# Seven block products for batch 1's second product, with other places for sums of w_out, for the scaling of second probabilities and for batch 3's softmax

## The chip, the cores and the metric

One NeuronCore of a Trainium2 chip runs the kernel. TensorE (PE) multiplies, VectorE (DVE), ScalarE (ACT) and GpSimd (POOL, Pool) work elementwise, SyncE (SP) issues most DMA transfers; each engine takes its own instructions in order. The metric is the device time of one execution in microseconds. Before the change the median of three runs was 206.49 us (206.39 to 206.8).

## The reference

x is (8, 8, 512, 64): batch, head, row, width; state is (8, 8, 32, 64). Two softmax attentions share their scores, and their results, stacked to 544 rows of 512 per batch, go through a two-layer product with a leaky ReLU.

```python
scale = 1.0 / np.sqrt(D)
scores = scale * np.matmul(x, state.transpose(0, 1, 3, 2))
scores = scores - scores.max(-1, keepdims=True)
a = np.exp(scores)
a /= a.sum(-1, keepdims=True) + 1e-09
xread = np.matmul(a, state)
scores2 = scale * np.matmul(state, x.transpose(0, 1, 3, 2))
scores2 = scores2 - scores2.max(-1, keepdims=True)
a2 = np.exp(scores2)
a2 /= a2.sum(-1, keepdims=True) + 1e-09
sread = np.matmul(a2, x)
attn = np.concatenate([xread, sread], axis=2)
x = attn.transpose(0, 2, 1, 3).reshape(B * S, H * D)   # S is 544 here
h = x @ w_in                                            # 512 x 2048
return np.maximum(0.01 * h, h) @ w_out                  # 2048 x 512
```

## The kernel before

Everything is in bf16 with sums in fp32. For a batch b the first product folds state and w_in together: M = state times w_in (`a_m`, four column groups of 512, numbered 0 to 3 here), so that the hidden layer is M applied to the first probabilities `aT`. M group c is computed into PSUM (tile `pm`) and copied to SBUF by `m_evict`.

The loop over s, 0 to 15, makes one 128-column block of the hidden layer per step: `ff1` runs two matmuls of 512 columns into a bank "ph" (two buffers, used in turn) and ScalarE's Prelu (L352) writes `hT[:, s]`. Each ff1 must wait until the Prelu two steps earlier, or whatever else used its bank, has emptied it.

Between the ff1 stand pieces of the second product, hT times w_out, of the batch before or of this batch. There are two ways of doing it:
- `piece(b, hT, i, jq)`: four matmuls of 512 columns for row block i and quarter jq of the depth, into a bank "py". 16 pieces make a batch; `y_store` copies a finished row block and sends it out. Batches 0 and 1 use this.
- `Batch` with `Fast`: the product is cut in 2 x 2 blocks, rows (256 + 256), depth (even and odd blocks of 128) and columns (256 + 256), and done with seven block products in place of eight. `Fast.sums` makes four sums of blocks of hT on VectorE (`su`, L511); `weights_sum` makes four sums of blocks of w_out (`tw`, L488, once for the kernel; sum 1 reads sum 2 and sum 3 reads sum 1). A unit (n, m) is two matmuls of 256 columns (L522), seven n times eight m for a batch. The products accumulate in two banks "py", in the order 1, 2, 6, 5, 7, 3, 4: 1, 6, 7 and 4 in the first, 2, 5, 3 in the second. Between them `save` copies a bank to SBUF on ScalarE (`sv`, L531) and `join` adds a bank to a saved block on VectorE (`yo`, L534). Batches 2 to 7 use this: 15 units of a batch run at the end of its own loop, 41 in the loop of the next, spread over the steps by `PACE`.

Other PSUM tags: "sc", one buffer of two banks, holds scores and sometimes a group of M; "big", one buffer of two banks, holds groups of M and the state reads (`psr`, L299).

Attention of the next batch is woven into the same loop: `a_scores` (TensorE), `a_shift` and `a_max2` (VectorE: transposed maximum L215, spread L223, subtraction L225, row maximum L265), `a_exp` and two `a_exp2` (ScalarE, L232 and L273), `a_probs` (VectorE, L237 to L247, writes `aT`), `a_probs2` (VectorE, L279 to L284: scales the second probabilities), `a_a2t` (a DMA transpose on SyncE's queue), `a_sread` (TensorE, then two ScalarE copies L306). `cast_x` makes bf16 of x on Pool (L105). a0, a1, a2 are the attention objects of batches 0 to 2.

The order of all instructions on each engine is the order in which the code issues them; semaphores follow from the tiles. So an instruction that waits holds all behind it on its engine.

Batch 1's loop is L858 to L885, the loops of batches 2 to 7 are L891 to L989. In batch 2's loop the ten remaining pieces of batch 1 are done at steps 0 to 9, groups 0, 1 and 2 of batch 3's M are computed after step 10, and group 2 is copied out of two "ph" banks by VectorE and ScalarE (L987):

```python
for g, copy in enumerate((VEC, SCA)):
    copy(nxt.M[:, g, 2 * DM:3 * DM], pm2[g][:])
```

Of the kernel before, what the change touches and what calls it, by code (L numbers as in the profile page):

```python
# [9 lines left out]
P = 128  # L10
# [17 lines left out]
def kernel(  # L28
# [248 lines left out]

    def a_probs2(a):
        nc.vector.tensor_scalar(out=a.r2[:], in0=a.r2[:], scalar1=1e-9, scalar2=None, op0=ALU.add)  # L279
        q2 = att.tile([P, 2], FP32, name="qc", tag="qc")  # L280
        nc.vector.reciprocal(q2[:], a.r2[:])
        a.a2 = att.tile([P, 2, S], BF16, name="a2", tag="a2")
        for g in range(2):
            nc.vector.tensor_scalar(  # L284
                out=a.a2[:, g, :], in0=a.e2[:, g, :],
                scalar1=q2[:, g:g + 1], scalar2=None, op0=ALU.mult,
            )

    def a_a2t(a):
# [54 lines left out]
    def ff1(a, hT, j):  # L344
        ph = psum.tile([P, S], FP32, name="ph", tag="ph")
        for g in range(2):
            nc.tensor.matmul(  # L347
                ph[:], lhsT=a.M[:, g, P * j:P * (j + 1)],
                rhs=a.aT[:, g, :],
                start=(g == 0), stop=(g == 1),  # L350
            )
        nc.scalar.activation(out=hT[:, j, :], in_=ph[:], func=AF.Prelu, alpha=0.01)  # L352


# [185 lines left out]
    class Batch:  # L540
        def __init__(self, b, hT):
            saved = {n: (spool, t, 1) for n, t in ((1, "sv1"), (6, "sv6"), (5, "sv1"), (7, "sv7"))}
            self.b, self.f = b, Fast(hT, 2 * P, [(spool, f"su{n}", 1) for n in range(4)], saved)
            self.units = [(n, m) for n in (1, 2, 6, 5, 7, 3, 4) for m in range(NM)]
            own = [(n, m) for n in (1, 2) for m in range(6)] + [(1, 6), (2, 6), (1, 7)]
            assert len(own) == OWN
            self.units = own + [u for u in self.units if u not in own]
            self.bank = {}
            self.yos = {}
# [22 lines left out]
        def run(self, count):  # L572
            f = self.f
            for _ in range(count):
                n, m = self.units.pop(0)
                if m == 0:
                    self.open(n)
                bank = self.bank[n]
                f.unit(bank, n, m, first=n in (1, 2, 5, 4))
                if m == NM - 1:  # L580
                    self.done(n, bank)

        def done(self, n, bank):
# [16 lines left out]
            elif n == 4:  # L600
                f.join(self.yo(1)[:, :, :HC], bank, 7)
                self.out(1)

    OWN = 15
    PACE = (1, 4, 4, 4, 3, 4, 4, 3, 4, 4, 4, 4, 3, 4, 3, 3)
    PACE2 = (0,) * 10 + (3, 3, 2, 2, 2, 3)

# [235 lines left out]
    open_xb(3)  # L843
    a_probs(a1)
    for i in range(NT):
        piece(0, h0, i, 2)
    for i in (2, 3):
        piece(0, h0, i, 3, copy=None)
    for i in (2, 3):
        y_store(0, i, VEC)  # L850
    for h in range(0, H, 2):
        cast_x(3, h, h + 2, POO)
# [5 lines left out]
    h1 = hpool.tile([P, 16, S], BF16, name="hT", tag="hT")  # L858
    fill = [(0, h0, 0, 3), (0, h0, 1, 3)] + [(1, h1, i, jq) for jq in range(3) for i in range(2)]
    for s in range(16):  # L860
        ff1(a1, h1, s)
        if s % 2:
            pb, hT, i, jq = fill[s // 2]
            piece(pb, hT, i, jq, copy=VEC if s == 3 else SCA)
        if s == 4:
            a_scores(a2)
            m_evict(a2, 0, a_m(a2, 0, "big"), SCA)
            a_shift(a2)
            a_max2(a2)
        elif s == 7:  # L870
            a_exp(a2)
            a_open(att_of[3], 3)
            a_xt_dma(att_of[3])
        elif s in (9, 11):
            a_exp2(a2, s // 2 - 4)
            if s == 9:
                a_probs(a2)
            else:
                a_probs2(a2)
        elif s == 13:  # L880
            a_probs2(a1)
            a_a2t(a1)
            pm = [a_m(a2, 1, "big"), a_m(a2, 2, "sc")]
            m_evict(a2, 1, pm[0], VEC)
            m_evict(a2, 2, pm[1], SCA)  # L885

    before = None
    weights_open()  # L890
    for b in range(2, B):  # L891
# [3 lines left out]
        now = Batch(b, hT)  # L895
        std = []
        if b == 2:
            std = [(i, 3) for i in range(2)] + [(i, jq) for i in range(2, NT) for jq in range(4)]

        def fill(s):  # L900
            n = (PACE2 if b == 2 else PACE)[s]
            left = min(n, len(before.units)) if before else 0
            if left:
# [4 lines left out]
        for s in range(16):  # L908
            if s == 11:
                fill(s)  # L910
            ff1(a, hT, s)
            if s == 0:
# [3 lines left out]
                a_a2t(a)  # L916
                if before:
                    for n in (0, 1):
                        before.f.sums(n, 4, 8)
            elif s == 1:  # L920
                if nxt is not None:
                    a_scores(nxt)
# [3 lines left out]
                if b + 2 < B:  # L926
                    for h in range(0, H, 2):
                        cast_x(b + 2, h, h + 2, POO)
                if before:
                    before.f.sums(2, 4, 8)  # L930
            elif s == 3:
                if before:
                    before.f.sums(3)
                if nxt is not None:
                    a_max2(nxt)
                if b == 2:
                    weights_sum(0)
                    weights_sum(2)
            elif s == 4:
                if b == 2:  # L940
                    load_state(1)
                    a_sread(a0)
            elif s == 6:
                if b == 2:
                    a_sread(a1)
            elif s == 8:
                a_sread(a)
                if b == 2:
                    state_t(1)
                    weights_sum(1)  # L950
                    weights_sum(3)
            elif s == 12:
                for n in range(3):
                    now.f.sums(n, 0, 4)
            if nxt is None:
                if s == 4:
# [3 lines left out]
                elif s == 10:  # L960
                    fi.w_sum(3)
                    fi.x_sums()
            if s == (11 if b == 2 else 7) and b + 2 < B:
                a_open(att_of[b + 2], b + 2)
                a_xt_dma(att_of[b + 2])
            if nxt is not None:
                if s == 5:
                    a_exp(nxt)
                elif s in (7, 8):
                    a_exp2(nxt, s - 7)  # L970
                    if s == 7:
                        a_probs(nxt)
                elif s == 11:
                    a_probs2(nxt)
                elif s in (12, 13):
                    SCA(nxt.M[:, s - 12, DM:2 * DM], pm1[:, s - 12, :])
            if std:
                i, jq = std.pop(0)
                piece(1, h1, i, jq)
            elif s != 11:  # L980
                fill(s)
            if s == 10 and nxt is not None:
                pm0 = a_m(nxt, 0, "big")
# [96 lines left out]
```

## Time and profile before

| what | value |
|---|---|
| median of three runs | 206.49 us |
| the profiled execution, its time | 206.1 us |
| its span, first to last instruction | 204.3 us |
| granted TensorE clock | 1.000 |
| ScalarE's Prelu of an ff1, L352, 112 | 603 ns each |
| ScalarE's exponential, L232, 128x1024, 7 | 1050 ns each |
| ScalarE's half exponentials, L273, 16 | 693 ns each |
| VectorE's half sums of hT, L511, 128x1024, 24 | 694 ns each |
| Pool's casts of x, L105, 128x512, 20 | 790 ns each |
| window 36.78 to 52.61 us (batch 1's loop): PE, DVE, ACT, POOL busy | 15.37, 13.83, 12.77, 2.30 us |
| window 52.61 to 74.61 us (batch 2's loop): PE, DVE, ACT, POOL busy | 22.00, 18.30, 18.14, 5.36 us |

A line of a timeline gives start, duration, engine, line and operation of the code, output and input by the program's names, sizes, and in brackets the idle time of that engine just before and what ended it. Matmuls overlap, so their rate is read from start to start; the ends of matmuls are modelled. Instructions in a row on one engine are merged with a count. The chain of waits follows the work that ended last back to its start.

### The profile page before, as it was taken

Reading aid. Unit: us, or ns where it says so; the run is one execution under the profiler, and the core shown is the slowest. Engines: PE = TensorE matmul, PEld = TensorE weight load, DVE = VectorE, ACT = ScalarE, POOL = GpSimd, SP = SyncE. Lnnn points to the kernel's source line nnn. Section 1 sums busy time; section 2 is a strip of 40 time slices with the busy share of each in tenths; the row PEclk is TensorE's granted clock in tenths of the full one; section 3 lists DMA queues with packets and bytes.
Section 4 is the critical chain, followed back from the end, with each engine's and each line's share of the span. In section 5 each row is a group of like instructions: output and inputs, shape, how many; then the busy total and the mean of one; then the engine's idle time right before and its main releaser. Section 6 shows DMA issues by size and latency. Waiting matters only on the chain.

```text
span 204.3 us, 4533 instructions
## 1 busy us (share of the span) xinstructions
PE 198.0 (97%) x1852; PEld 126.8 (62%) x1852; DVE 152.3 (75%) x231; ACT 145.2 (71%) x274; POOL 41.8 (20%) x66
## 2 busy tenths in 40 slices
PE   7899999999999999999999999999999999999992
PEld 2543534443445557766776767776767677799882
DVE  1677689599699969966996699679978763686622
ACT  3359848578959796978787878788778856467710
POOL 8921002021035103500402040200020002004250
PEclk9999999999999999999999999999999999999999
DMA  5999994799456498549452769250016000410035
GB/s 188 223 207 280 227 253 134 147 305 218 104 179 176 128 194 176 53 155 269 95 103 106 209 152 106 99 160 5 0 47 210 3 3 22 183 55 0 3 90 167
DMA packets 38772, 27.74 MB, mean 136 GB/s; under 512 B 24352, under 2 KB 35744, under 8 KB 38752
## 3 DMA queue, kind: packets, MB, share of 16 engines
q1 hardware_dynamic: 33552, 20.65, 40.0%
q0 software_dynamic: 4912, 6.55, 15.7%
q8 instruction: 14, 0.23, 0.4%
q10 hardware_dynamic: 288, 0.26, 0.4%
q14 instruction: 6, 0.05, 0.1%
HBM read 17.30 MB, written 8.91 MB: 128 GB/s over the span
## 4 chain that ended last, share of the span: by engine, by line
PE 93%; DVE 3%; ACT 1%; issue 0%; ACTq 0%
PE yq L522 36%; PE ph L347 23%; PE py L452 9%; PE pm L326 4%; PE pyw L452 3%; PE pf L406 3%; PE yu L522 3%; PE pspin L132 2%; PE ph L768 2%; PE psr L299 2%; PE sc L205 1%; PE php L768 1%; DVE mrow L215 1%; DVE mrowb L223 1%; DVE sh L225 1%; DVE M L340 1%
## 5 line engine op out<-in xcount | busy, mean ns | idle before, releaser
L352 ACT ACTIVATE hT<-ph 128x512 bf16<-128x512 f32 x112 | 65.7, 603 | 22.5 <-PE ph L347 22.0
L347 PE MATMUL ph<-aT,M 128*128 128x512 bf16 x224 | 64.6, 379 | 0.5 <-ACT hT L352 0.5
L522 PEld LDWEIGHTS <-su 128*128 128x128 bf16 x416 | 39.4, 98 | 13.5 <-DVE su L511 1.7
L522 PEld LDWEIGHTS <-hT 128*128 128x128 bf16 x288 | 27.7, 98 | 12.8 <-issue 2.1
L347 PEld LDWEIGHTS <-M 128*128 128x128 bf16 x224 | 21.7, 98 | 10.9 <-issue 1.7
L105 POOL CAST xb<-xl 128x512 bf16<-128x512 f32 (+1 forms) x21 | 16.0, 802 | 57.6 <-DMA xl<-in_x_dram 33.1
L522 PE MATMUL yq<-tw_xf,su 128*128 128x256 bf16 x192 | 27.2, 273 | 0.0
L522 PE MATMUL yq<-w_out_bf,hT 128*128 128x256 bf16 x192 | 27.0, 273 | 0.0
L511 DVE TENSOR_TENSOR su<-hT 128x1024 bf16<-128x1024 bf16 x24 | 16.7, 694 | 10.5 <-ACT hT L352 10.5
L452 PE MATMUL py<-w_out_bf,hT 128*128 128x512 bf16 x96 | 24.2, 379 | 0.0
L452 PEld LDWEIGHTS <-hT 128*128 128x128 bf16 x128 | 11.9, 98 | 14.3 <-issue 1.3
L592 POOL TENSOR_TENSOR yo<-sv,sv 128x512 f32<-128x512 f32 x6 | 7.8, 1303 | 56.0 <-ACT sv L531 41.0
L534 DVE TENSOR_TENSOR yo<-yq,sv 128x512 f32<-128x512 f32 x17 | 11.6, 685 | 6.5 <-PE yq L522 6.5
L531 ACT COPY sv<-yq 128x512 f32<-128x512 f32 x24 | 13.9, 585 | 2.0 <-PE yq L522 1.4
L340 ACT CAST M<-pm 128x1024 bf16<-128x1024 f32 x13 | 13.2, 1014 | 0.6 <-PE pm L326 0.6
L522 PE MATMUL yq<-w_out_bf,su 128*128 128x256 bf16 x96 | 13.1, 273 | 0.0
L522 PE MATMUL yq<-tw_x,su 128*128 128x256 bf16 x96 | 13.1, 272 | 0.0
L522 PE MATMUL yq<-tw_x,hT 128*128 128x256 bf16 x88 | 12.1, 273 | 0.0
L273 ACT ACTIVATE e<-sc,mcols 128x512 bf16<-128x512 f32 x16 | 11.0, 693 | 0.1
L215 DVE TRANSPOSE_TENSOR_REDUCE mrow<-sc 128x32 f32<-128x1024 f32 x7 | 8.7, 1244 | 2.4 <-PE sc L205 2.3
L265 DVE TENSOR_REDUCE mcol<-sc 128x2 f32<-128x1024 f32 x8 | 9.7, 1215 | 0.0
L246 DVE STREAM_TRANSPOSE qb<-qh 128x1024 bf16<-128x1024 bf16 x7 | 8.7, 1246 | 0.2
(142 smaller groups left out, 272.7 us busy)
## 6 DMA issues: line engine op xcount, KB each, us to landing
xl<-in_x_dram SPq DMA_DIRECT2D x5, 1024.0 KB, 7.0
out_dram<-yo SPq DMA_DIRECT2D x10, 512.0 KB, 2.8
w_in_bf<-in_moe_w_in_dram POOLq DMA_DIRECT2D x4, 512.0 KB, 9.2
w_out_bf<-in_moe_w_out_dram POOLq DMA_DIRECT2D x4, 512.0 KB, 17.1
out_dram<-ysb SPq DMA_DIRECT2D x8, 256.0 KB, 4.6
xf<-in_x_dram SPq DMA_DIRECT2D x2, 512.0 KB, 4.8
x<-in_x_dram POOLq DMA_DIRECT2D x2, 512.0 KB, 13.9
xl<-in_x_dram POOLq DMA_DIRECT2D x1, 1024.0 KB, 18.6
```

The source lines that it names most:

```text
L105: copy(xs[b][:, :, h0:h1].rearrange("p t h d -> p h t d"), xl[b][:, h0:h1].rearrange("p h (t d) -> p h t d", t=NT),)
L215: nc.vector.tensor_reduce(out=m1[:], in_=flat.rearrange("p (c j) -> p c j", j=NS), axis=AX.X, op=ALU.max, apply_transpose=True,)
L265: nc.vector.tensor_reduce(out=m2[:], in_=a.sc[:], axis=AX.X, op=ALU.max, negate=True)
L273: nc.scalar.activation(out=a.e2[:, g], in_=a.sc[:, g, :], func=AF.Exp, bias=a.m2s[:, g:g + 1], scale=SCALE, accum_out=a.r2[:, g:g + 1],)
L340: copy(a.M[:, :, cols], pm[:])
L347: nc.tensor.matmul(ph[:], lhsT=a.M[:, g, P * j:P * (j + 1)], rhs=a.aT[:, g, :], start=(g == 0), stop=(g == 1),)
L352: nc.scalar.activation(out=hT[:, j, :], in_=ph[:], func=AF.Prelu, alpha=0.01)
L452: nc.tensor.matmul(y.py, lhsT=hT[:, j, P * i:P * (i + 1)], rhs=w_out_bf[:, j, :], start=(j == 0), stop=(j == 15),)
L511: (eng or nc.vector).tensor_tensor(out=S[n][:, ms], in0=u[:, ms], in1=v[:, ms], op=op)
L522: nc.tensor.matmul(bank[:, i, :], lhsT=lhs[:, m, P * i:P * (i + 1)], rhs=rhs[:, m, :], start=(first and m == 0 and (i == 0 or of is not No ...
L531: copy(t[:], bank)
L534: nc.vector.tensor_tensor(out=dst, in0=bank, in1=self.sv[n][:], op=ALU.add)
```

## The change

- Batch 1's second product is done by `Batch` too. 14 units of products 1 and 2 (m from 0 to 6, alternating) run in batch 1's loop by `PACE1`, two more after it, 40 in batch 2's loop. For batch 1 product 4 is accumulated onto product 7 in its bank, and ScalarE's copy replaces the last join.
- In batch 1's loop steps 6 and 7, and 10 and 11, become pairs (`ff1_pair`): four matmuls into the two banks of "big" and one Prelu of 128x1024. The scores of batch 2 move from step 4 to 5, its exponential from 7 to 9, its half exponentials from 9 and 11 to 11 and 13. Pieces of batch 0 stand at steps 1 and 3.
- Sums 2 and 1 of w_out are made before batch 1's loop (in the order 2, 1), sums 0 and 3 early in batch 2's loop.
- For batches 1 and 2 Pool scales the second probabilities (`a_scale2`), after VectorE's `a_norm2`.
- In batch 2's loop the scores of batch 3 move from step 1 to 3, its exponential from 5 to 8, its half exponentials from 7 and 8 to 10 and 11, its first probabilities from 7 to 10; the groups of M for batch 3 are computed after step 12 in place of 10 (`ses`). Its second probabilities and three half sums of hT are now issued at step 12, ahead of the copies of M. ScalarE evicts both groups 1 and 2 of batch 2's M, at steps 0 and 1. The state reads move to steps 5, 7 and 10.
- Loops of batches 3 to 7 keep their order.

```diff
@@ -275,16 +275,22 @@
             bias=a.m2s[:, g:g + 1], scale=SCALE, accum_out=a.r2[:, g:g + 1],
         )
 
-    def a_probs2(a):
+    def a_norm2(a):
         nc.vector.tensor_scalar(out=a.r2[:], in0=a.r2[:], scalar1=1e-9, scalar2=None, op0=ALU.add)
-        q2 = att.tile([P, 2], FP32, name="qc", tag="qc")
-        nc.vector.reciprocal(q2[:], a.r2[:])
+        a.q2 = att.tile([P, 2], FP32, name="qc", tag="qc")
+        nc.vector.reciprocal(a.q2[:], a.r2[:])
+
+    def a_scale2(a, eng):
         a.a2 = att.tile([P, 2, S], BF16, name="a2", tag="a2")
         for g in range(2):
-            nc.vector.tensor_scalar(
+            eng.tensor_scalar(
                 out=a.a2[:, g, :], in0=a.e2[:, g, :],
-                scalar1=q2[:, g:g + 1], scalar2=None, op0=ALU.mult,
+                scalar1=a.q2[:, g:g + 1], scalar2=None, op0=ALU.mult,
             )
+
+    def a_probs2(a):
+        a_norm2(a)
+        a_scale2(a, nc.vector)
 
     def a_a2t(a):
         a.a2T = att.tile([P, 2, NT, P], BF16, name="a2T", tag="a2T")
@@ -350,6 +356,16 @@
                 start=(g == 0), stop=(g == 1),
             )
         nc.scalar.activation(out=hT[:, j, :], in_=ph[:], func=AF.Prelu, alpha=0.01)
+
+    def ff1_pair(a, hT, j, tag):
+        ph = psum.tile([P, 2, S], FP32, name="phw", tag=tag, bufs=1)
+        for v in range(2):
+            for g in range(2):
+                nc.tensor.matmul(
+                    ph[:, v], lhsT=a.M[:, g, P * (j + v):P * (j + v + 1)], rhs=a.aT[:, g, :],
+                    start=(g == 0), stop=(g == 1),
+                )
+        nc.scalar.activation(out=hT[:, j:j + 2, :], in_=ph[:], func=AF.Prelu, alpha=0.01)
 
 
     class FastIn:
@@ -542,8 +558,10 @@
             saved = {n: (spool, t, 1) for n, t in ((1, "sv1"), (6, "sv6"), (5, "sv1"), (7, "sv7"))}
             self.b, self.f = b, Fast(hT, 2 * P, [(spool, f"su{n}", 1) for n in range(4)], saved)
             self.units = [(n, m) for n in (1, 2, 6, 5, 7, 3, 4) for m in range(NM)]
-            own = [(n, m) for n in (1, 2) for m in range(6)] + [(1, 6), (2, 6), (1, 7)]
-            assert len(own) == OWN
+            if b == 1:
+                own = [(n, m) for m in range(NM - 1) for n in (1, 2)]
+            else:
+                own = [(n, m) for n in (1, 2) for m in range(6)] + [(1, 6), (2, 6), (1, 7)]
             self.units = own + [u for u in self.units if u not in own]
             self.bank = {}
             self.yos = {}
@@ -576,7 +594,7 @@
                 if m == 0:
                     self.open(n)
                 bank = self.bank[n]
-                f.unit(bank, n, m, first=n in (1, 2, 5, 4))
+                f.unit(bank, n, m, first=n in (1, 2, 5) + ((4,) if self.b > 1 else ()))
                 if m == NM - 1:
                     self.done(n, bank)
 
@@ -598,12 +616,15 @@
                 f.join(self.yo(0)[:, :, HC:], bank, 6)
                 self.out(0, slice(HC if self.b == B - 1 else 0, DM))
             elif n == 4:
-                f.join(self.yo(1)[:, :, :HC], bank, 7)
+                if self.b > 1:
+                    f.join(self.yo(1)[:, :, :HC], bank, 7)
+                else:
+                    SCA(self.yo(1)[:, :, :HC], bank)
                 self.out(1)
 
-    OWN = 15
     PACE = (1, 4, 4, 4, 3, 4, 4, 3, 4, 4, 4, 4, 3, 4, 3, 3)
-    PACE2 = (0,) * 10 + (3, 3, 2, 2, 2, 3)
+    PACE1 = (0, 0, 0, 0, 1, 1, 1, 1, 2, 1, 1, 1, 1, 2, 1, 1)
+    PACE2 = (0,) + PACE[1:]
 
     att_of = [Attn() for _ in range(B)]
     a0, a1, a2 = att_of[:3]
@@ -842,12 +863,15 @@
     load_x(3, nc.sync)
     open_xb(3)
     a_probs(a1)
+    weights_open()
+    weights_sum(2)
     for i in range(NT):
         piece(0, h0, i, 2)
     for i in (2, 3):
         piece(0, h0, i, 3, copy=None)
     for i in (2, 3):
         y_store(0, i, VEC)
+    weights_sum(1)
     for h in range(0, H, 2):
         cast_x(3, h, h + 2, POO)
     a_probs2(a0)
@@ -856,57 +880,60 @@
 
 
     h1 = hpool.tile([P, 16, S], BF16, name="hT", tag="hT")
-    fill = [(0, h0, 0, 3), (0, h0, 1, 3)] + [(1, h1, i, jq) for jq in range(3) for i in range(2)]
+    before = Batch(1, h1)
     for s in range(16):
-        ff1(a1, h1, s)
-        if s % 2:
-            pb, hT, i, jq = fill[s // 2]
-            piece(pb, hT, i, jq, copy=VEC if s == 3 else SCA)
-        if s == 4:
+        if s in (6, 10):
+            ff1_pair(a1, h1, s, "big")
+        elif s not in (7, 11):
+            ff1(a1, h1, s)
+        if s == 5:
             a_scores(a2)
             m_evict(a2, 0, a_m(a2, 0, "big"), SCA)
             a_shift(a2)
             a_max2(a2)
-        elif s == 7:
-            a_exp(a2)
+        if s in (1, 3):
+            piece(0, h0, (3 - s) // 2, 3, copy=VEC if s == 3 else SCA)
+        before.run(PACE1[s])
+        if s == 7:
             a_open(att_of[3], 3)
             a_xt_dma(att_of[3])
-        elif s in (9, 11):
-            a_exp2(a2, s // 2 - 4)
-            if s == 9:
-                a_probs(a2)
-            else:
-                a_probs2(a2)
-        elif s == 13:
-            a_probs2(a1)
-            a_a2t(a1)
-            pm = [a_m(a2, 1, "big"), a_m(a2, 2, "sc")]
-            m_evict(a2, 1, pm[0], VEC)
-            m_evict(a2, 2, pm[1], SCA)
-
-
-
-    before = None
-    weights_open()
+        elif s == 9:
+            a_exp(a2)
+            a_norm2(a1)
+            before.f.sums(0, 0, 4)
+            a_probs(a2)
+            a_scale2(a1, nc.gpsimd)
+        elif s in (11, 13):
+            a_exp2(a2, s // 2 - 5)
+    before.f.sums(1, 0, 4)
+    before.run(2)
+    pm = [a_m(a2, 1, "big"), a_m(a2, 2, "sc")]
+    for n in (0, 1):
+        before.f.sums(n, 4, 8)
+    a_norm2(a2)
+    a_scale2(a2, nc.gpsimd)
+    a_a2t(a1)
+
+
+
     for b in range(2, B):
         hT = hpool.tile([P, 16, S], BF16, name="hT", tag="hT")
         a = att_of[b]
         nxt = att_of[b + 1] if b + 1 < B else None
         now = Batch(b, hT)
-        std = []
-        if b == 2:
-            std = [(i, 3) for i in range(2)] + [(i, jq) for i in range(2, NT) for jq in range(4)]
+        two = b == 2
+        ses = 12 if two else 10
 
         def fill(s):
-            n = (PACE2 if b == 2 else PACE)[s]
-            left = min(n, len(before.units)) if before else 0
+            n = (PACE2 if two else PACE)[s]
+            left = min(n, len(before.units))
             if left:
                 before.run(left)
             if n > left:
                 now.run(n - left)
 
         for s in range(16):
-            if s == 11:
+            if s == ses + 1:
                 fill(s)
             ff1(a, hT, s)
             if s == 0:
@@ -914,10 +941,18 @@
                     load_x(b + 2, nc.sync)
                     open_xb(b + 2)
                 a_a2t(a)
-                if before:
+                if two:
+                    m_evict(a, 1, pm[0], SCA)
+                else:
                     for n in (0, 1):
                         before.f.sums(n, 4, 8)
             elif s == 1:
+                if two:
+                    m_evict(a, 2, pm[1], SCA)
+                    weights_sum(0)
+                    before.f.sums(2)
+                    before.f.sums(3)
+            if s == (3 if two else 1):
                 if nxt is not None:
                     a_scores(nxt)
                 m_evict(a, 3, a_m(a, 3, "big"), SCA)
@@ -926,32 +961,31 @@
                 if b + 2 < B:
                     for h in range(0, H, 2):
                         cast_x(b + 2, h, h + 2, POO)
-                if before:
+                if two:
+                    weights_sum(3)
+                    a_max2(nxt)
+                else:
                     before.f.sums(2, 4, 8)
             elif s == 3:
-                if before:
-                    before.f.sums(3)
+                before.f.sums(3)
                 if nxt is not None:
                     a_max2(nxt)
-                if b == 2:
-                    weights_sum(0)
-                    weights_sum(2)
             elif s == 4:
-                if b == 2:
+                if two:
                     load_state(1)
+            elif s == 5:
+                if two:
                     a_sread(a0)
-            elif s == 6:
-                if b == 2:
+            elif s == 7:
+                if two:
                     a_sread(a1)
-            elif s == 8:
-                a_sread(a)
-                if b == 2:
-                    state_t(1)
-                    weights_sum(1)
-                    weights_sum(3)
+            elif s == 8 and two:
+                state_t(1)
             elif s == 12:
                 for n in range(3):
                     now.f.sums(n, 0, 4)
+            if s == (10 if two else 8):
+                a_sread(a)
             if nxt is None:
                 if s == 4:
                     fi = FastIn(None)
@@ -960,26 +994,23 @@
                 elif s == 10:
                     fi.w_sum(3)
                     fi.x_sums()
-            if s == (11 if b == 2 else 7) and b + 2 < B:
+            if s == (11 if two else 7) and b + 2 < B:
                 a_open(att_of[b + 2], b + 2)
                 a_xt_dma(att_of[b + 2])
             if nxt is not None:
-                if s == 5:
+                if s == (8 if two else 5):
                     a_exp(nxt)
-                elif s in (7, 8):
-                    a_exp2(nxt, s - 7)
-                    if s == 7:
+                elif s in ((10, 11) if two else (7, 8)):
+                    a_exp2(nxt, s - (10 if two else 7))
+                    if s == (10 if two else 7):
                         a_probs(nxt)
-                elif s == 11:
+                elif s == (12 if two else 11):
                     a_probs2(nxt)
-                elif s in (12, 13):
-                    SCA(nxt.M[:, s - 12, DM:2 * DM], pm1[:, s - 12, :])
-            if std:
-                i, jq = std.pop(0)
-                piece(1, h1, i, jq)
-            elif s != 11:
+                elif s in (ses + 2, ses + 3):
+                    SCA(nxt.M[:, s - ses - 2, DM:2 * DM], pm1[:, s - ses - 2, :])
+            if s != ses + 1:
                 fill(s)
-            if s == 10 and nxt is not None:
+            if s == ses and nxt is not None:
                 pm0 = a_m(nxt, 0, "big")
                 pm1 = a_m(nxt, 1, "sc")
                 pm2 = a_m(nxt, 2, "ph")
```

## The prediction

> **What bounds the kernel now.** I read the page's first table, then its chain, then TensorE's list of waits.
>
> ```profile
> PE 198.0 (97%) x1852; PEld 126.8 (62%) x1852; DVE 152.3 (75%) x231; ACT 145.2 (71%) x274; POOL 41.8 (20%) x66
> ...
> PE 93%; DVE 3%; ACT 1%; issue 0%; ACTq 0%
> ```
>
> ```profile
> PE ph L347 <- ACT hT L352: 0.5, 1, 0.5
> ```
>
> TensorE works nearly without a break, and after the start its only wait for another engine is 0.5 us long. So a saving of TensorE work shows in full, but only while the others keep pace. The stages touched are batch 1's loop (first matmul at 36.78 us, next batch's first at 52.61: 15.83 us) and batch 2's (52.61 to batch 3's first at 74.61: 22.00 us). The timeline of the first:
>
> ```profile
> 40.98 0.40 PE L326 MATMUL pm<-w_in_bf,st_t 64*32 64x512 bf16 x8
> ...
> 41.52 1.01 ACT L340 CAST M<-pm 128x1024 bf16<-128x1024 f32 x1
> ...
> 43.51 1.02 PE L452 MATMUL py<-w_out_bf,hT 128*128 128x512 bf16 x4
> ...
> 45.12 1.06 ACT L232 ACTIVATE e<-sh 128x1024 bf16<-128x1024 f32 x1 [0.79 <-DVE sh L225]
> ...
> 46.72 1.08 PE L347 MATMUL ph<-aT,M 128*128 128x512 bf16 x4 [0.46 <-ACT hT L352]
> ```
>
> The 0.5 us arise because ScalarE's exponential (1.06) stands ahead of the activations that free TensorE's two "ph" banks. The eviction of M (41.52 to 42.53) holds the "big" bank pair, and costs nothing now because the next user of "big" comes ten microseconds later. The second stage:
>
> ```profile
> 69.58 0.83 PE L522 MATMUL yq<-w_out_bf,hT 128*128 128x256 bf16 x6
> 69.71 0.69 DVE L987 CAST M<-pm 128x512 bf16<-128x512 f32 x1 [0.22 <-PE pm L326]
> ...
> 70.38 1.02 PE L347 MATMUL ph<-aT,M 128*128 128x512 bf16 x4
> ```
>
> Here VectorE was idle and took the M copy the moment that TensorE had finished; its release of a "ph" bank at 70.40 falls inside the next product, which shows no wait.
>
> **The change on TensorE.** Removed: 64 matmuls of 512 columns; four take 0.87 us from start to start (37.64 to 38.51), so 13.86 in all. Added: 7 x 8 x 2 = 112 of 256 columns, eight in 0.87, so 12.2. Gain 1.66. With the 0.46 wait gone too, 2.1 us is the most that can come out. A unit (two matmuls) is 0.218, an ff1 0.433.
>
> **Batch 1's loop, laid end to end.** TensorE's own work there is now 16 ff1 (6.93), 2 pieces (1.73), 16 units (3.48), scores and three groups of M (1.1), some 0.2 of gaps at changes of shape: 13.45. ScalarE starts an activation 0.63 after its ff1 starts, successive ones 0.48 apart (two in 1.09), a 1024-wide one some 0.93 apart (1.03 each, L778), an exponential of a half 0.66.
> - Steps 0 to 5 without waits: ff1 of step 5 at 40.89, scores 41.42, M group 0 ("big") 41.64 to 41.98, one unit to 42.20. Step 6 is a pair that writes "big", and must wait for the eviction: ScalarE takes the activation of step 5 at 41.52, then the 1.01 us eviction from 42.18 to about 43.2. TensorE stands 1.0 us with one unit of cover where before it had a piece and four steps.
> - The second pair (step 10) starts at 46.04 and ends at 46.9. ScalarE: the exponential of batch 2 from 46.5, the pair's activation from 47.47, half an exponential from 48.4, then the activations of steps 12 (49.06) and 13. Step 13's unit needs the pair: 0.1 lost. Step 14 needs step 12's bank, free at 49.7, but TensorE is there at 48.98: 0.7. The other half exponential precedes the activations of 14 and 15 (50.68, 51.16), which the two units after the loop read: 0.3 and 0.3.
> - Sum of stalls 2.45. Batch 2's first ff1 comes at 52.7, against 52.61, with as much TensorE work left as before (40 units, 8.7, for 10 pieces, 8.66).
>
> VectorE meanwhile: both moved sums (L488, 1.2 to 1.6 each) fit behind aT at 36.04: 37.3, two copies to 38.5, the second sum to 39.7, a0's probabilities to 40.6, a copy to 41.3, scores visible at 41.6. So moving them is free, hidden by VectorE's idle 0.9 and 1.2 us there. Its max, spread and shift end at 45.4, the exponential's result is read from 47.8, aT of batch 2 is done at 51.6: 1.1 before its reader.
>
> **Batch 2's loop.** ScalarE now evicts M groups 1 and 2 between the activations of steps 0, 1 and 2: bank "sc" is free at 56.2, wanted at 56.17, so nothing. The copies of saved blocks (L531, 0.585 x 4) replace ysb copies of like cost. VectorE, free-running after 51.6: half sum 0.7, join 0.65, two half sums 1.4, normalisation 0.35, w_out sum 1.2, two full sums of 1.22, max, spread and shift 3.75, w_out sum 1.2 to 1.5, max and scale 1.4: about 64.4. Next in its queue is the join of block 3, and that needs its eighth unit, in step 9: TensorE issues it at 65.79, so the join starts at 66.0. Behind it stand, in this order, the probabilities of batch 3, three half sums, a3's second probabilities, and only then the copy of M (L987) that frees a "ph" bank:
>
> ```profile
> 62.97 1.23 DVE L237 TRANSPOSE_TENSOR_REDUCE r<-e 128x32 f32<-128x1024 bf16 x1
> 64.23 0.18 DVE L241 TENSOR_SCALAR r<-r 128x32 f32<-128x32 f32 x1
> 64.45 0.35 DVE L244 RECIPROCAL qh<-r 128x32 bf16<-128x32 f32 x1
> 64.83 1.25 DVE L246 STREAM_TRANSPOSE qb<-qh 128x1024 bf16<-128x1024 bf16 x1
> 66.11 0.69 DVE L247 TENSOR_TENSOR aT<-e,qb 128x1024 bf16<-128x1024 bf16 x1
> ```
>
> From start to start: join 0.60, these five 3.75, three half sums 1.93 (71.24 to 73.2), normalisation 0.39 and scaling 0.53, copy 0.69: 7.9, so the bank is free at 73.9. TensorE's work between the same unit and that bank's next user, ff1 of step 14, is: two units 0.43; step 10, 0.43 + 0.57 (state read) + 0.87; step 11, 1.30; step 12, 1.08 and three groups of M 0.87; four units 0.87 and ff1 13, 0.43: 6.85, so it is there at 72.65 and waits 1.3. Before, nothing stood ahead of that copy. Behind it wait step 14's activation and everything of batch 3. The remaining two steps (2.17) bring batch 3's first ff1 to 76.1, against 74.61: **1.5 us later**, with the work after it as it was.
>
> **The queues passed.** SyncE issues a1's transpose earlier, once Pool has scaled (by 50), then x of batch 4 as now (53.3). The transpose of a2 waits for a0's state read (59.8), as before (59.55), and lands 5.1 later, before its reader at 66.7. load_state follows it at 61, now 61.94. Nothing here reaches TensorE.
>
> **Pool's four scalings** (128x512) are in no row: from below a cast of that size undisturbed, 2.29 / 4 = 0.57, from above the sum of two tensors, 1.30. I take 0.6, the one-input row. They take 0.62 per batch off VectorE, but can hold its additions:
>
> ```profile
> 107.19 1.27 POOL L592 TENSOR_TENSOR yo<-sv,sv 128x512 f32<-128x512 f32 x1 [5.93 <-issue]
> ```
>
> ```profile
> 107.78 1.22 DVE L247 TENSOR_TENSOR aT<-e,qb 128x1024 bf16<-128x1024 bf16 x1
> ```
>
> aT takes 0.69 alone and 1.22 here. Batch 2's two scalings (from 54.6) fall on VectorE's w_out sum and full sums: 0 to 2.6 lost, and the casts of batch 4 perhaps 0.4. VectorE has 66.0 - 64.4 = 1.6 to spare before the join; 2 x 0.6 + 0.4 uses just that. So 0 in the sum, up to 1.4 in the range. The Trainium skill, "SBUF — State Buffer", section "SBUF: two separate sides", says that VectorE operations with two SBUF inputs and GpSimd share one port pair as an exclusive lock for a whole instruction, the loser blocked. By that, aT above would end at 108.46 + 0.69 = 109.15; it ended at 109.00, so the trace nearly agrees, and by the rule with the dear Pool row the change would cost 1.4 more.
>
> **Sum.** Span 204.3 + 1.5 = 205.8; with the 1.8 outside it (206.1 - 204.3) 207.6 for that execution. The median of the runs shown is 0.39 above it, so **208.0 us**.
>
> **Rivals.**
> 1. *ScalarE keeps pace in batch 1's loop* (not slower). If the order of activations let TensorE through, 2.45 would come back there. For: ScalarE is busy 71%, pairs save overhead. Against: a single-buffered "big" with 0.22 of cover. But VectorE's free-running chain would then decide from about 1.4 us of lead on: its join at 64.5, copy at 72.4, batch 3 at 74.6, so 206.5: no change.
> 2. *TensorE stays the bound throughout*: 206.5 - 1.66 - 0.46 = 204.4. Against: it needs VectorE's 7.9 under TensorE's 6.85 and no ScalarE wait.
> 3. *Pool's lock makes VectorE late to the join*: up to 2 x 1.3 + 0.4 - 1.6 = 1.4 more, 209.4; it decides once the scalings take over 0.6 each.
>
> That the seven products are not there can be ruled out: the matmuls are counted above.
>
> **Chances.** Forecast 0.50 (own range 207.2 to 208.8), rival 1 0.18, rival 2 0.14, rival 3 0.18. The range 205.3 to 209.6 leaves out most of rival 2 and the far end of rival 3. A measurement can't tell less than 0.2% (0.4 us) from no change: faster 0.17 (rival 2, a little of 1), same 0.15, slower 0.68.
>
> **What would show it.** Right: TensorE idle about 1 us ahead of the first pair for ScalarE's eviction, some 1.4 us in steps 13 to 15, batch 2's first ff1 near 52.7, and one wait of 1.0 to 1.6 us for VectorE's copy of M near 73 us, batch 3 starting near 76. Wrong: TensorE without these waits, VectorE idle ahead of that copy, or a loss in a later batch. Pool scalings over 0.9 us, and no idle ahead of the join of block 3, would speak for rival 3.

## The result and the profile after

The changed kernel takes 207.74 us (median of 6 runs, 207.32 to 208.09) beside 206.48 us for the kernel before on the same chip (6 runs, 206.28 to 206.8): a ratio of 1.006, 95% interval 1.0046 to 1.0075. The change makes the kernel slower by 0.6%. Forecast were 208.0 us, and a span of 205.8 us; the profiled execution's span is 205.8 us.

The page's first table and its chain, which answer to those of before:

```profile
PE 196.7 (96%) x1900; PEld 131.2 (64%) x1900; DVE 155.7 (76%) x234; ACT 146.4 (71%) x274; POOL 49.4 (24%) x71
...
PE 82%; DMA 5%; DVE 5%; ACT 3%; POOL 2%; issue 1%; POOLq 0%; DVEq 0%
```

TensorE is busy for 1.3 us less, as fewer columns are multiplied, and yet the span is 1.5 us longer: VectorE and ScalarE now have shares in the chain that ended last, 5% and 3% where it was 3% and 1%. (The 5% of DMA and 2% of Pool are the loads at the very start, which the chain of this execution happens to follow.) TensorE's waits by line, the three that concern the change:

```profile
PE ph L353 <- DVE M L1018: 1.4, 1, 1.4
...
PE phw L364 <- ACT M L346: 0.9, 1, 0.9
PE ph L353 <- ACT hT L358: 0.5, 1, 0.5
```

Each column is the total, the number of times and the longest. One wait of 0.5 became three of 2.8 together, with a fourth of 0.2 for the units behind batch 1's loop. In the timeline of TensorE they stand here (the window from 36 us):

```profile
41.88 0.39 PE L538 MATMUL yq<-w_out_bf,hT 128*128 128x256 bf16 x2
43.15 1.02 PE L364 MATMUL phw<-aT,M 128*128 128x512 bf16 x4 [0.87 <-ACT M L346]
...
49.61 0.59 PE L353 MATMUL ph<-aT,M 128*128 128x512 bf16 x2 [0.54 <-ACT hT L358]
...
51.26 0.88 PE L538 MATMUL yq<-w_out_bf,hT 128*128 128x256 bf16 x4 [0.19 <-ACT hT L358]
...
52.62 1.04 PE L353 MATMUL ph<-aT,M 128*128 128x512 bf16 x4
...
71.91 0.59 PE L353 MATMUL ph<-aT,M 128*128 128x512 bf16 x2
73.86 0.59 PE L353 MATMUL ph<-aT,M 128*128 128x512 bf16 x2 [1.36 <-DVE M L1018]
...
76.03 0.59 PE L353 MATMUL ph<-aT,M 128*128 128x512 bf16 x2
```

The first wait is the pair of step 6, which needs "big"; the next two are step 14 and the units behind the loop; 52.62 is batch 2's first ff1 (before: 52.61). At 73.86 stands step 14 of batch 2's loop, and 76.03 is batch 3's first ff1 (before: 74.61). The bracket counts idle time from the modelled end of the work before. From the end of issue (41.88 + 0.22, 71.91 + 0.43) the waits are 1.05 and 1.52 us. Nearly all of the loss is made in batch 2's loop: batch 1's takes 15.92 us in place of 15.83, batch 2's 76.03 - 52.62 = 23.41 in place of 22.00. By the clock batch 3 starts 76.03 - 74.61 = 1.42 later.

VectorE in the same stretch, from its timeline:

```profile
65.82 0.69 DVE L550 TENSOR_TENSOR yo<-yq,sv 128x512 f32<-128x512 f32 x1 [0.36 <-PE yq L538]
...
69.59 0.69 DVE L247 TENSOR_TENSOR aT<-e,qb 128x1024 bf16<-128x1024 bf16 x1
70.20 0.68 DVE L527 TENSOR_TENSOR su<-hT 128x1024 bf16<-128x1024 bf16 x1
70.92 0.69 DVE L527 TENSOR_TENSOR su<-su,hT 128x1024 bf16<-128x1024 bf16 x1
71.52 0.68 DVE L527 TENSOR_TENSOR su<-hT 128x1024 bf16<-128x1024 bf16 x1
72.12 0.16 DVE L279 TENSOR_SCALAR r<-r 128x2 f32<-128x2 f32 x1
72.39 0.17 DVE L281 RECIPROCAL qc<-r 128x2 f32<-128x2 f32 x1
72.59 0.61 DVE L286 TENSOR_SCALAR a<-e,qc 128x512 bf16<-128x512 bf16 x2
73.12 0.68 DVE L1018 CAST M<-pm 128x512 bf16<-128x512 f32 x1
```

The join can't start before TensorE's unit; from there VectorE doesn't rest, and the copy that TensorE needs comes last, 7.98 us after the join's start. 2.9 us of that (70.20 to 73.12) are work that nobody waits for yet.

### The profile page after: what moved, and what is told of

The parts are those of the page before. It is cut to its first block, busy times and chain, and to the rows that moved or that the text cites. A ratio compares the mean times of both kernels' runs of the same rounds, so it can differ in the third digit from the quotient of the medians.

```text
span 205.8 us, 4642 instructions
## 1 busy us (share of the span) xinstructions
PE 196.7 (96%) x1900; PEld 131.2 (64%) x1900; DVE 155.7 (76%) x234; ACT 146.4 (71%) x274; POOL 49.4 (24%) x71
## 4 chain that ended last, share of the span: by engine, by line
PE 82%; DMA 5%; DVE 5%; ACT 3%; POOL 2%; issue 1%; POOLq 0%; DVEq 0%
PE yq L538 39%; PE ph L353 21%; DMA w_in_bf<-in_moe_w_in_dram 5%; PE py L468 3%; PE pyw L468 3%; PE pm L332 3%; PE pf L422 3%; PE yu L538 3%; PE ph L789 2%; PE psr L305 2%; ACT hT L358 1%; PE sc L205 1%; DVE su L527 1%; POOL w_in_bf L118 1%; ACT e L273 1%
## 5 line engine op out<-in xcount | busy, mean ns | idle before, releaser
L538 PEld LDWEIGHTS <-su 128*128 128x128 bf16 x480 | 45.4, 98 | 15.9 <-DVE su L527 1.3
L538 PE MATMUL yq<-w_out_bf,hT 128*128 128x256 bf16 x224 | 32.4, 273 | 0.3 <-ACT hT L358 0.2
L538 PE MATMUL yq<-tw_xf,su 128*128 128x256 bf16 x224 | 31.5, 273 | 0.0
L527 DVE TENSOR_TENSOR su<-hT 128x1024 bf16<-128x1024 bf16 (+1 forms) x27 | 19.2, 710 | 11.3 <-ACT hT L358 11.3
L547 ACT COPY sv<-yq 128x512 f32<-128x512 f32 x28 | 16.3, 588 | 2.0 <-PE yq L538 1.4
L538 PE MATMUL yq<-tw_x,su 128*128 128x256 bf16 x112 | 15.3, 273 | 0.0
L538 PE MATMUL yq<-w_out_bf,su 128*128 128x256 bf16 x112 | 15.3, 273 | 0.0
L538 PE MATMUL yq<-tw_x,hT 128*128 128x256 bf16 x104 | 14.3, 273 | 0.0
L527 DVE TENSOR_TENSOR su<-su,hT 128x1024 bf16<-128x1024 bf16 x14 | 9.7, 691 | 0.4
L286 POOL TENSOR_SCALAR a<-e,qc 128x512 bf16<-128x512 bf16 x4 | 8.5, 2124 | 4.3 <-ACT M L346 3.9
```

The costliest lines, as they stand in the source:

```text
L527: (eng or nc.vector).tensor_tensor(out=S[n][:, ms], in0=u[:, ms], in1=v[:, ms], op=op)
L538: nc.tensor.matmul(bank[:, i, :], lhsT=lhs[:, m, P * i:P * (i + 1)], rhs=rhs[:, m, :], start=(first and m == 0 and (i == 0 or of is not No ...
L547: copy(t[:], bank)
```

## The experiments

Ratios are to the kernel before, run on the same chip in the same hour. The changed kernel's own is 1.006. The loop of batch 1 does not begin at the same time in every trace: its first ff1 stands at 36.78 us in the kernel before, at 36.70 in the changed one, and at 36.29 to 36.84 in those of the experiments. Where two traces are compared below, "from the loop's start" means that times are counted from that ff1. Batch 3 starts 37.83 us from the loop's start in the kernel before and 39.33 in the changed one.

**1. The copy of M first.** In batch 2's loop the half sums and the second probabilities are issued behind the copies of M:

```diff
-            elif s == 12:
+            elif s == 12 and not two:
                 for n in range(3):
                     now.f.sums(n, 0, 4)
...
-                elif s == (12 if two else 11):
+                elif s == 11 and not two:
                     a_probs2(nxt)
...
                 m_evict(nxt, 0, pm0, SCA)
+                if two:
+                    for n in range(3):
+                        now.f.sums(n, 0, 4)
+                    a_probs2(nxt)
```

> The changed kernel with one order mended: in batch 2's loop the three half sums and the second probabilities of batch 3 are issued after VectorE's copy of M, not ahead of it. Theory (the copy stands behind 2.9 us of VectorE work and holds the 'ph' bank of step 14): TensorE's wait of 1.36 us at step 14 goes, batch 3's first ff1 comes at 74.7 in place of 76.0, time 207.7 - 1.3 = 206.4, the same as before the change. Rival (VectorE's queue is the bound as a whole, so whatever is pushed back meets TensorE a little later): the wait comes back at the half sums of batch 3's loop and the time stays at 207.4 to 207.8.

Measured: 206.1 us beside 206.24, ratio 0.9992 (0.9981 to 1.0003). VectorE's timeline of this kernel:

```profile
71.23 0.69 DVE L1018 CAST M<-pm 128x512 bf16<-128x512 f32 x1 [0.88 <-PE pm L332]
71.83 0.68 DVE L527 TENSOR_TENSOR su<-hT 128x1024 bf16<-128x1024 bf16 x1
```

and TensorE's:

```profile
71.98 1.03 PE L353 MATMUL ph<-aT,M 128*128 128x512 bf16 x4
...
74.59 0.59 PE L353 MATMUL ph<-aT,M 128*128 128x512 bf16 x2
```

VectorE now idles 0.88 us for the copy's input, steps 13 and 14 run as one group of four matmuls, and batch 3 begins at 74.59, 37.82 from the loop's start. The half sums, 1.6 us later than in the changed kernel, hold nobody up. The theory stands, the rival falls: this order alone is the whole difference between slower and no change.

**2. The reverse: the same order put into the kernel before.** Only the half sums and second probabilities of batch 2's loop move, to ahead of the copies (L986):

```diff
-            elif s == 12:
+            elif s == 12 and b > 2:
...
-                elif s == 11:
+                elif s == 11 and b > 2:
                     a_probs2(nxt)
...
                 pm2 = a_m(nxt, 2, "ph")
+                if b == 2:
+                    for n in range(3):
+                        now.f.sums(n, 0, 4)
+                    a_probs2(nxt)
                 for g, copy in enumerate((VEC, SCA)):
```

> The kernel before the change, with only one order altered: in batch 2's loop the three half sums and the second probabilities of batch 3 are issued ahead of VectorE's copy of M. Theory (the price is the VectorE work put ahead, as far as TensorE has no other cover): the copy ends near 73.0 in place of 70.4, TensorE waits 2.2 us for it at step 12, time 208.4. Rival (that order is harmless and the loss of the change lies in the seven products or in Pool): 206.2 to 206.5.

Measured: 208.29 us beside 206.23, ratio 1.0103 (1.009 to 1.0116). TensorE's timeline of this kernel:

```profile
73.04 0.59 PE L347 MATMUL ph<-aT,M 128*128 128x512 bf16 x2 [1.65 <-DVE M L991]
```

The wait is in its place and the time as expected. The trace shows 1.65 in place of 2.2: from the end of issue (the ff1 before starts at 70.80) it is 1.81, and in this execution TensorE was already 0.42 us late there (70.80 for 70.38) after a wait for a transpose (0.51 at batch 2's scores).

**3. Two singles for the first pair**, so that step 6 needs no "big":

```diff
-        if s in (6, 10):
+        if s == 10:
             ff1_pair(a1, h1, s, "big")
-        elif s not in (7, 11):
+        elif s != 11:
             ff1(a1, h1, s)
```

> The changed kernel with steps 6 and 7 of batch 1's loop as two single ff1 in the 'ph' banks in place of one pair in 'big'. Theory (batch 2's stall is set by VectorE's chain from the join on, and VectorE waits only 0.36 us for TensorE there): the 0.87 us wait ahead of the pair goes and batch 2 starts near 51.8 in place of 52.6, but TensorE only waits longer at step 14 (1.8 in place of 1.36); time 207.3 to 207.4. Rival (stalls add up): 0.87 less, 206.9.

Measured: 207.04 us beside 206.24, ratio 1.0046 (1.0033 to 1.006), an interval that overlaps the changed kernel's. By the clock batch 3 starts 0.32 us earlier (75.71), but the loop started 0.24 earlier too: from the loop's start only 0.08 is gained (39.25 for 39.33). TensorE's timeline:

```profile
51.96 1.02 PE L353 MATMUL ph<-aT,M 128*128 128x512 bf16 x4 [0.20 <-DVE aT L247]
...
54.49 1.05 PE L538 MATMUL yq<-tw_xf,su 128*128 128x256 bf16 x8 [0.20 <-DVE su L527]
...
73.54 0.59 PE L353 MATMUL ph<-aT,M 128*128 128x512 bf16 x2 [1.36 <-DVE M L1018]
```

The size is the theory's, the mechanism is not. Batch 2 starts 0.42 earlier from the loop's start (15.50 for 15.92), but the gain is lost right behind it, to VectorE's probabilities and half sums (0.20 and 0.20), so the wait at step 14 stays at 1.36 us. I had read the 0.36 us ahead of the join as all of VectorE's rest. It is not, as the small scale ahead of it (L267) shows; here with Pool's addition, from the two engines' timelines of the changed kernel:

```profile
64.17 1.27 POOL L610 TENSOR_TENSOR yo<-sv,sv 128x512 f32<-128x512 f32 x1 [1.94 <-ACT sv L547]
...
64.47 1.00 DVE L267 TENSOR_SCALAR mcols<-mcol 128x2 f32<-128x2 f32 x1
```

The scale takes 0.17 us where Pool does nothing. Here it takes 1.00 and ends at 65.47, just behind Pool's addition (65.44); in this run and in those of experiments 4 and 9 it takes 0.62, 0.63 and 0.46, and ends 0.02 to 0.04 behind that addition each time. So it is held for Pool, and what is held is rest: VectorE could have come to the scale some 1.2 us later (64.47 + 0.17 to 65.82) without moving the join, which waits for TensorE.

Pool has a part in the lost gain as well. In this trace the scale (46.58) and the half sum (47.14) of batch 1's loop take 0.38 and 0.90 us while Pool casts x, where the trace of experiment 5 has 0.17 and 0.67. The casts start when a load has landed, so how much of this an execution shows depends on the load.

**4. Both edits.**

> Both edits of the two other kernels. Theory: with VectorE's copy out of the way the 0.8 us of batch 1's loop shows in full, 1.36 + 0.8 less, batch 3's first ff1 near 73.9, time 205.6, faster than before the change by 0.9. Rival (VectorE bound as a whole): no better than the first of the two, 206.4 or more.

Measured: 206.02 us beside 206.24, ratio 0.9995 (0.9982 to 1.0007). A miss: the theory's 205.6 isn't reached. Batch 3's first ff1 comes at 74.08, which from the loop's start is only 0.11 ahead of experiment 1 (37.71 for 37.82): the gain of batch 1's loop is lost at batch 2's start as in experiment 3, to waits of 0.22 and 0.20 for VectorE. Then comes another wait:

```profile
75.97 0.41 PE L205 MATMUL sc<-xT,st_t 64*32 64x512 bf16 x8 [0.65 <-DMA xT<-xb]
```

The next to be late is a DMA. SyncE's queue issues the transpose of batch 4's x behind the transpose of its state, which waited for Pool's cast of it, and that for its load. That cast began at 68.28 here and at 66.85 in experiment 1, where the scores did not wait. So this wait hangs on when the load lands, and one trace does not show how many executions have it.

**5. That transpose earlier**, at step 7 in place of 11, ahead of the state's:

```diff
-            if s == (11 if two else 7) and b + 2 < B:
+            if s == 7 and b + 2 < B:
```

> The kernel with both edits (copy first, singles), and the transpose of batch 4's x issued at step 7 of batch 2's loop in place of 11, so ahead of the transpose of batch 4's state and of an output on SyncE's queue. Theory (with VectorE's wait gone the next to end last is that transpose, for which TensorE stood 0.65 us at batch 3's scores): that wait goes, 0.6 less than the kernel with both edits, 205.4, and faster than before the change. Rival (the state's transpose, now behind it, is late in its place, or the gain is eaten by VectorE's half sums): 206.0.

Measured: 205.79 us beside 206.23, ratio 0.9975 (0.9965 to 0.9986). The 0.65 us wait is gone, scores at 75.26 in place of 75.97. The median lies between theory and rival, but the interval is on the side of faster than before the change. Against experiment 4 the two intervals just overlap (0.9982 to 0.9986), and not all of the difference between the two traces is the edit's: batch 2 already starts 15.19 from the loop's start in place of 15.47, since in experiment 4 a small instruction of VectorE (L279) took 0.61 in place of 0.16 us while Pool cast x. What the edit alone is worth is open.

**6. Three more moves in batch 1's loop:**

```diff
     a_a2t(a0)
+    a_norm2(a1)
+    a_scale2(a1, nc.gpsimd)
...
-        elif s in (11, 13):
-            a_exp2(a2, s // 2 - 5)
+        elif s == 11:
+            a_exp2(a2, 0)
     before.f.sums(1, 0, 4)
+    a_exp2(a2, 1)
     before.run(2)
-    pm = [a_m(a2, 1, "big"), a_m(a2, 2, "sc")]
+    pm = [a_m(a2, 1, "big")]
```

besides the half sum behind `a_probs(a2)` and group 2 in batch 2's step 1.

> As the kernel with x's transpose early, and three more moves in batch 1's loop: VectorE's normalisation and Pool's scaling of a1 ahead of the loop, its first half sum behind the probabilities of batch 2, and ScalarE's second half exponential behind the activations of steps 14 and 15 (with group 2 of batch 2's M then in batch 2's step 1). Theory (at batch 2's start VectorE's probabilities and half sums and ScalarE's exponentials are what TensorE waits for, 0.20, 0.20, 0.54 and 0.19 us): aT comes 0.8 earlier, batch 2 starts near 51.2, another 0.5 to 0.8 less, 204.6 to 204.9. Also Pool's scaling, then beside VectorE work that reads PSUM, shows whether its 1.7 us were its own or VectorE's doing. Rival: ScalarE's load bounds batch 1's loop whatever the order, 205.4.

Measured: 205.5 us beside 206.23, ratio 0.9967 (0.9954 to 0.998). Less than expected: aT is done at 50.59 in place of 51.80, batch 2 starts at 51.25 as forecast and batch 3 at 73.60. From the loop's start that is 0.43 and 0.13 earlier than in experiment 5 (14.76 for 15.19, 37.11 for 37.24), and against it the intervals overlap. ScalarE's two waits (0.54 and 0.25) are still there.

**7. The first half exponential later too** (`a_exp2(a2, 0)` at step 13).

> As the kernel with the three more moves in batch 1's loop, and the first half exponential of batch 2 after the activations of steps 12 and 13 too. Theory (TensorE's last waits there, 0.54 us at step 14 and 0.25 us after the loop, are the place of the half exponentials in ScalarE's queue): the 0.54 goes, batch 2 starts near 50.8, 205.0 to 205.1. Rival (ScalarE is loaded so far that the wait moves to the units behind steps 14 and 15): 205.4 to 205.6.

Measured: 205.63 us beside 206.47, ratio 0.9967 (0.9954 to 0.9979): no gain. The 0.54 at step 14 is gone and batch 2 starts at 50.59, from the loop's start 0.46 earlier (14.30 for 14.76), but not far on TensorE waits for VectorE's second half sums:

```profile
53.80 1.05 PE L538 MATMUL yq<-tw_xf,su 128*128 128x256 bf16 x8 [0.43 <-DVE su L527]
```

Neither theory nor rival: the wait moved to VectorE, not to ScalarE's units.

**8. One part alone: two sums of w_out ahead,** in the kernel before.

> The kernel before the change, with one part of it alone: sums 2 and 1 of w_out made ahead of batch 1's loop. Theory (hidden in VectorE's idle time of 0.9 and 1.2 us there): no change, 206.1 to 206.5. Rival: the copies of batch 0's last rows behind them make the pieces or the scores late, 0.3 to 1 us slower.

Measured: 206.36 us beside 206.23, ratio 1.0007 (0.9991 to 1.0022); TensorE's waits behind the start are as before. Free, as forecast.

**9. The scalings on VectorE again,** in the changed kernel:

```diff
-            a_scale2(a1, nc.gpsimd)
+            a_scale2(a1, nc.vector)
...
-    a_scale2(a2, nc.gpsimd)
+    a_scale2(a2, nc.vector)
```

> The changed kernel with the second probabilities of batches 1 and 2 scaled on VectorE again. Theory (VectorE lost little to Pool: one sum of 1.63 in place of 1.22, one small scale of 1.00 in place of 0.2): VectorE gains these 1.2 back and pays two scalings of 0.53, so the join starts within 0.3 us of 65.8 and the time is the same, 207.5 to 208.0. Rival (Pool's long instructions, 2.1 us each, hold VectorE): the join and with it step 14 come about 1 us earlier, 206.7.

Measured: 207.49 us beside 206.24, ratio 1.0059 (1.0045 to 1.0073), as the changed kernel's. VectorE reaches its small scale ahead of the join at 65.41 in place of 64.47, and the join waits for TensorE in both. Counted from the last line of batch 2's probabilities (L247, at 51.33 and 51.11) that is 14.08 in place of 13.36, so Pool's part of the change gives VectorE some 0.7 us, and the kernel nothing.

**10. What one scaling takes on Pool,** four additional ones in the kernel before, with an unused result.

> The kernel before the change with four additional scalings of a 128x512 bf16 tile on Pool in a stretch (20 to 30 us) where Pool is idle and VectorE mostly reads PSUM; their result is not used. Measures what one scaling takes by itself. Theory A (Pool's 1.6 to 2.5 us in the changed kernel are its own speed): 1.5 us or more each here. Theory B (they were stretched by VectorE's two-input additions): 0.6 to 0.8 each. Time 206.2 to 206.5 either way.

Measured: 206.34 us beside 206.47, ratio 1.0 (0.9987 to 1.0012). The line's durations, least, median and most:

```profile
L809 POOL TENSOR_SCALAR a<-idle,warm x4: 1552/1568/1756, 16.5 to 21.2; 128x512 bf16<-128x512 bf16 x4
```

Theory A: some 1.57 us is the scaling's own time. Pool's first two scalings in experiment 6 agree, with 3.12 us for both.

## Why the prediction was right, point by point

- **TensorE's gain of 1.66.** TensorE is busy 1.3 us less by the page (198.0 to 196.7), a sum that counts overlaps and modelled ends; the columns that are left out are certain, the exact 1.66 was not isolated by a run. That a gain is there is seen where waits are removed: with the mended orders of experiment 6 batch 3 starts 0.72 us earlier from the loop's start than before the change (37.11 for 37.83), though waits of 0.79 (0.54 and 0.25) are left, against 0.46 before. That makes 1.05; the rest of the 1.66 is not shown.
- **Batch 1's loop.** Forecast 15.92 us from first ff1 to batch 2's first; measured 52.62 - 36.70 = 15.92. The wait for "big" was put at 1.0 (1.05 from the end of issue), that of step 14 at 0.7 (49.61 - 48.45 - 0.44 = 0.72), those of the two units behind the loop at 0.3 each (51.26 - 50.69 - 0.22 = 0.35, and 0.28, as four such matmuls take 0.88 in place of 0.60). So each stall came where it was laid out. Without the pair's wait batch 2 starts 0.42 and 0.45 earlier from the loop's start (experiments 3 and 4) and 0.73 earlier in experiment 5, whose loop is the same: not all of a removed wait comes out.
- **Batch 2's loop.** Join at 66.0 forecast, 65.82 measured; copy done at 73.9, 73.80; batch 3 at 76.1, 76.03. TensorE came to step 14 at 72.34, 0.3 earlier than the 72.65 laid out, so the wait was 1.5 in place of 1.3; that changes nothing, as the copy decides. VectorE's terms ahead of the join add up to 64.7 to 65.0 and not to 64.4 as written; measured it is at the scale at 64.47, as its lines follow each other faster than their lengths (55.65 to 56.78 for a sum of 1.22). Experiments 1 and 2 show cause and price from both sides: out, the time of before; in, 2.06 us on the kernel before.
- **No cost on the queues passed, and none for the sums moved ahead.** Experiment 8 shows the second. The first held in the changed kernel, where TensorE was late, and also in experiment 1's trace, where batch 3 starts as early as before the change. In experiment 4's trace, with the load of batch 4's state landing later, the queue did reach TensorE (0.65 us). So the sentence that nothing there reaches TensorE was right for the forecast, with less to spare than it sounded.
- **Pool's scalings: the mis-sized term.** The bracket was 0.57 to 1.30 us and the value taken 0.6; alone they take 1.57, and in the changed kernel 1.56 to 3.45. The rival that hung on them nevertheless fell. It was to decide above 0.6 us each, by holding VectorE's additions, and by the prediction's own working 2 x 1.57 + 0.4 - 1.6 would have put the join 1.9 us late. That the 0 in the sum came out is luck: VectorE lost 0.41 on one full sum (1.63 for 1.22, and 1.22 again in experiment 9, without Pool's scalings), and the join still waited for TensorE. Of the two signs named for that rival one came (scalings over 0.9 us) and the other did not (0.36 us of idle time stand ahead of the join). In the timelines of VectorE and of Pool:

```profile
54.52 1.21 DVE L504 TENSOR_TENSOR tw_xf<-w_out_bf 128x2048 bf16<-128x2048 bf16 x1
55.65 1.22 DVE L527 TENSOR_TENSOR su<-hT 128x2048 bf16<-128x2048 bf16 x1
56.78 1.63 DVE L527 TENSOR_TENSOR su<-hT,su 128x2048 bf16<-128x2048 bf16 x1
...
54.76 5.08 POOL L286 TENSOR_SCALAR a<-e,qc 128x512 bf16<-128x512 bf16 x2 [3.85 <-ACT M L346]
```

VectorE came first at 54.52, Pool's first scaling started at 54.76, and it was Pool that stretched, two scalings in 5.08 us where two alone take 3.1. By the Trainium skill, "SBUF — State Buffer", section "SBUF: two separate sides", whoever starts first holds the shared ports for its whole instruction. The trace agrees that the later comer waits (3.45 us for Pool's first scaling is 1.55 and 1.9 of waiting). It also shows what the sentence alone would not tell: VectorE's second addition (55.65) goes at full speed beside a scaling that is shown as begun at 54.76. And the third (56.78) lost only 0.41, though that scaling went on to 58.21, so a hold for the whole of it is not what this trace shows.
- **The other rivals.** That ScalarE keeps pace in batch 1's loop is refuted by TensorE's three waits for it (0.87, 0.54 and 0.19). That TensorE stays the bound was to give 2.1 us less than before; experiment 6, which comes nearest, reached 0.7 (205.5 beside 206.23), with ScalarE's two waits still in it. What would be left without any wait of the two stages is open.
- **From the span to the median.** The profiled execution was forecast at 207.6 and took 207.6. The median was put 0.39 above it, as in the kernel before, and was 0.14 above it: that is the 0.26 between 208.0 and 207.74.

The version of experiment 6 beats both kernels: 0.9967 of the time before, that is 0.3% faster, and 0.9% faster than the changed kernel by the quotient of the ratios (0.9967 / 1.006).

## What to carry to other kernels

A saving on the engine that is busy 97% shows only if each release that it needs is as early in the other engines' queues as before. When steps are moved, read each engine's new order from the last thing that waits for TensorE to the first thing TensorE waits for, and add up what stands between: here 7.9 us of VectorE against 6.85 of TensorE told the loss in the traces (1.42 us) to within 0.1 us. The mend cost nothing: the copy that frees a bank goes first, and work whose reader is a batch away goes behind it.

## What the runs showed of the hardware

Pool's multiplication of a 128x512 bf16 tile by a value per partition takes 1.57 us, nearly three times its cast of a tile of the same size from fp32 (0.57) and more than its sum of two fp32 tiles (1.30). And Pool can hold even a very small VectorE instruction: the 128x2 scale (L267) takes 0.17 us where Pool does nothing. It took 0.23 to 1.00 in 19 places of these traces, and in 18 of them it ended 0.02 to 0.04 us after an instruction of Pool's that had begun before it; in the kernel before, for one, it ran from 59.87 to 60.38 beside a cast that ended at 60.36. (The other place is beside a scaling of experiment 10, with 0.40.) So a short instruction with a long time in a trace can be a wait for the other engine and not work, and the idle time shown behind it is then too small as a measure of rest.
